# Decay of the state by small DMAs instead of column sums, with a new order of all engines, in a linear-attention and maxout kernel

## The chip, the cores and the metric

The kernel runs on one core of a Trainium2 chip. The metric is device time in microseconds (us) of one execution. Each quoted time is a median of several executions. A "step" below is the period of TensorE (PE) from one tile to the next, read between the transposes of x (`xtp`) of two neighbouring tiles.

## The reference, cut to what matters

A gated linear attention runs over 768 positions for 4 batches and 8 heads of 48 channels. Its output goes, as 3072 rows of 384, through a maxout layer of width 1024.

```python
f = 1.0 / (1.0 + np.exp(-f_logit))
for t in range(S):
    state = f[:, :, t, :, None] * state + np.einsum('bhd,bhe->bhde', k[:, :, t], v[:, :, t])
    y[:, :, t] = np.einsum('bhd,bhde->bhe', q[:, :, t], state)
x = y.transpose(0, 2, 1, 3).reshape(B * S, H * D)
out = np.maximum(x @ w1, x @ w2) @ w_out
```

## The kernel before

The sequence is cut into 6 chunks of 128 positions; chunk and batch make 24 tiles. For each tile the kernel forms `cum`, the running sum of -log f within the chunk, by one matmul with a triangle of ones. Then `ei` = exp(cum) scales k into `kp`, and `ed` = exp(-cum) scales q into `qp`. The state that goes into the next chunk is multiplied by the decay of the whole chunk, `fl`. It comes from column sums, four matmuls with one column each, which put the channels on partitions, where the state update wants them:

```python
    def p_cum(i):
        ...
        nc.tensor.matmul(out=ps[:, 0:dm], lhsT=ut, rhs=ell[:, :, 0:D], start=True, stop=True)
        for p in range(NP if i // B < nch - 1 else 0):
            nc.tensor.matmul(out=ps[:, dm + p:dm + p + 1], lhsT=ell[:, 2 * p:2 * p + 2, :]..., rhs=ones_col, ...)
    def a_ed(i):
        t = st[i]["ed"] = work.tile([C, dm], F32, name="ed", tag="ed")
        nc.scalar.activation(t, psum["cum", i][:, 0:dm], AF.Exp, scale=-1.0)
    def a_fl(i):
        ...
        nc.scalar.activation(t, psum["cum", i][:, dm:dm + NP], AF.Exp, scale=-1.0)
    def m_st(i):        # on GpSimd: new state = (old state + k'v) * fl
        ...
    def v_v(i):         # on VectorE: v to bf16
        nc.vector.tensor_copy(vb, ld[i]["v"].rearrange("p h d -> p (h d)"))
```

The order on every engine is written out by hand. A steady step is this list; a name is an operation and the number is its tile, relative to the current one. `lf`, `lk`, `lq`, `lv` are loads of 192 KB and `out` is a store, all issued by SyncE. `kpv` is kp on VectorE and `qp` is qp on GpSimd. `e` and `ln` make -log f. `tr` transposes kp and qp (copied to `trs`), `a` multiplies the two, `am` is `a` times the causal mask, `y` is am times v plus q times the old state, and `x` is y in bf16. `xT` transposes x, `d` is x times wd = w1 - w2, `g` its ReLU, and `o` the output row block, from g times w_out and x times w2o = w2 w_out, since max(a, b) = b + ReLU(a - b). `sa`, `tmp` and `st` update the state.

```python
STEP = """
st -4  d0 -1  cum 1  a 0  ed 1  d1 -1  g0 -1  am 0  lv 2  qp 1  fl 1  ei 1  lq 3  g1 -1
o0 -1  kpv 1  y 0  tmp -2  lk 3  o1 -1  x 0  e 2  xT 0  tr 1  ln 2  out -4  xTe 0  sa -1
tre 1  ob -1  lf 4  v 1
"""
```

A PROLOGUE and an EPILOGUE, written the same way, hold the first seven and the last few tiles.

## Time and profile before

| | kernel before |
|---|---|
| median of 3 runs | 146.11 us (146.02 to 146.57) |
| span of the profiled run | 144.2 us, granted clock 1.00 |
| step, middle and late | 4.98 and 4.90 us |
| busy: PE, VectorE (DVE), ScalarE (ACT), GpSimd (POOL) | 90%, 72%, 61%, 38% |

The prediction below shows the lines on which the reading of this kernel rests. The busy table of one stretch of the steady state (columns: stretch, length, then busy time and instruction count of each engine, granted clock, DMA share, GB/s):

```profile
85.00:120.00 35.00, 35.00 (x527) 28.35 (x525) 27.77 (x50) 23.60 (x57) 15.97 (x22) 1.00 0.98 206
```

PE is busy for all 35 us, and the DMA share is 0.98, at 206 GB/s. (The share adds up the times of all packets over 16 engines and can pass 1.) The list of DMA issues (columns: tiles, issuing engine, count, size, and median time from issue to landing):

```profile
ft<-in_f_logit_dram SPq DMA_DIRECT2D x24, 192.0 KB, 4.2
vt<-in_v_dram SPq DMA_DIRECT2D x24, 192.0 KB, 4.5
```

A load takes over 4 us from the start of its issue to its landing, although one is issued every us. So some four DMAs of SyncE's queue are under way at any time (3.4 on average, counted from the end of an issue; see below).

### The profile page before, as it was taken

Reading aid. Unit: us, or ns where it says so; the run is one execution under the profiler, and the core shown is the slowest. Engines: PE = TensorE matmul, PEld = TensorE weight load, DVE = VectorE, ACT = ScalarE, POOL = GpSimd, SP = SyncE. Lnnn points to the kernel's source line nnn. Section 1 sums busy time; section 2 is a strip of 40 time slices with the busy share of each in tenths; the row PEclk is TensorE's granted clock in tenths of the full one; section 3 lists DMA queues with packets and bytes.
Section 4 is the critical chain, followed back from the end, with each engine's and each line's share of the span. In section 5 each row is a group of like instructions: output and inputs, shape, how many; then the busy total and the mean of one; then the engine's idle time right before and its main releaser. Section 6 shows DMA issues by size and latency. Waiting matters only on the chain.

```text
span 144.2 us, 4442 instructions
## 1 busy us (share of the span) xinstructions
PE 130.0 (90%) x1820; PEld 101.3 (70%) x1820; DVE 104.4 (72%) x191; ACT 88.6 (61%) x199; POOL 54.6 (38%) x80
## 2 busy tenths in 40 slices
PE   0197499999899999999999999999999999999981
PEld 0044366677678877887887788778878877777771
DVE  7234988766989778877977797798779777976520
ACT  3572548877387566658566765766585667663440
POOL 8320060230556066236524632652364246362000
PEclk9999999999999999999999999999999999999999
DMA  4999999999999999999898999989899998971111
GB/s 93 271 362 386 341 303 154 188 188 140 206 174 196 188 213 221 173 227 233 166 203 183 215 208 210 219 181 196 182 198 222 190 251 180 225 223 57 59 55 55
DMA packets 104612, 28.60 MB, mean 198 GB/s; under 512 B 100368, under 2 KB 103568, under 8 KB 104592
## 3 DMA queue, kind: packets, MB, share of 16 engines
q1 hardware_dynamic: 104592, 28.32, 90.1%
q8 instruction: 14, 0.23, 0.7%
q14 instruction: 6, 0.05, 0.1%
HBM read 23.59 MB, written 4.72 MB: 196 GB/s over the span
## 4 chain that ended last, share of the span: by engine, by line
PE 72%; SPq 19%; DMA 4%; DVE 1%; issue 1%; ACT 0%
PE o L352 25%; PE d L334 22%; SPq L148 13%; PE tr L249 6%; PE a L267 5%; SPq L153 5%; DMA vt<-in_v_dram 4%; PE y L312 3%; PE y L307 2%; PE xtp L322 2%; PE cum L214 2%; PE sa L281 2%; SPq L157 1%; PE o L373 1%; DVE am L272 1%
## 5 line engine op out<-in xcount | busy, mean ns | idle before, releaser
L242 POOL TENSOR_TENSOR qp<-qt,ed 128x384 bf16<-128x384 f32 x22 | 22.3, 1013 | 61.7 <-ACT ed L226 31.6
L334 PE MATMUL d<-xT,wd 128*128 128x128 bf16 x576 | 40.6, 220 | 0.8 <-DVE xT L326 0.4
L352 PE MATMUL o<-wo,gT 128*128 128x384 bf16 x184 | 37.4, 325 | 0.0
L334 PEld LDWEIGHTS <-wd 128*128 128x128 bf16 x576 | 34.4, 114 | 3.8 <-DVE wd L175 0.6
L341 ACT ACTIVATE gT<-d 128x512 bf16<-128x512 f32 x48 | 29.0, 604 | 10.1 <-PE d L334 10.0
L272 DVE TENSOR_TENSOR am<-a,mask 128x1024 bf16<-128x1024 f32 x24 | 29.4, 1224 | 0.7 <-PE a L267 0.7
L296 POOL TENSOR_TENSOR st<-tmp,fl 64x192 bf16<-64x192 f32 x40 | 25.5, 638 | 1.6
L326 DVE COPY xT<-xtp 128x384 bf16<-128x384 bf16 x24 | 8.6, 358 | 21.1 <-PE xtp L322 21.1
L352 PEld LDWEIGHTS <-gT 128*128 128x128 bf16 x184 | 16.1, 97 | 9.1 <-ACT gT L341 0.2
L226 ACT ACTIVATE ed<-cum 128x384 f32<-128x384 f32 x24 | 11.8, 493 | 16.5 <-PE cum L216 13.1
L258 DVE COPY trs<-tr 128x1024 bf16<-128x1024 bf16 (+1 forms) x27 | 17.0, 631 | 2.9 <-PE tr L249 1.1
L317 ACT CAST x<-y 128x384 bf16<-128x384 f32 x24 | 11.5, 478 | 12.3 <-PE y L312 12.3
L352 PE MATMUL o<-w2o,xT 128*128 128x384 bf16 x69 | 15.0, 326 | 0.0
L201 ACT ACTIVATE e<-ft 128x384 f32<-128x384 f32 x24 | 12.5, 525 | 3.4 <-DMA ft<-in_f_logit_dram 3.4
L237 DVE TENSOR_TENSOR kp<-kt,ei 128x384 bf16<-128x384 f32 x23 | 14.1, 613 | 0.5 <-ACT ei L222 0.5
L214 PE MATMUL cum<-ell,ut 128*128 128x384 bf16 x24 | 8.1, 340 | 6.8 <-ACT ell L205 6.8
L205 ACT ACTIVATE ell<-e 128x384 bf16<-128x384 f32 x24 | 12.5, 524 | 0.7
L357 DVE COPY ob<-o 128x384 f32<-128x384 f32 x23 | 12.6, 548 | 0.0
L222 ACT ACTIVATE ei<-cum 128x384 f32<-128x384 f32 x24 | 12.1, 503 | 0.0
L312 PE MATMUL y<-vb,am 128*128 128x48 bf16 x192 | 11.3, 183 | 0.8 <-DVE am L272 0.6
L312 PEld LDWEIGHTS <-am 128*128 128x128 bf16 x192 | 9.6, 96 | 3.1 <-DVE am L272 1.4
L289 DVE TENSOR_TENSOR tmp<-sa,st 128x384 f32<-128x384 f32 x20 | 10.9, 546 | 0.0
(56 smaller groups left out, 167.6 us busy)
## 6 DMA issues: line engine op xcount, KB each, us to landing
ft<-in_f_logit_dram SPq DMA_DIRECT2D x24, 192.0 KB, 4.2
qt<-in_q_dram SPq DMA_DIRECT2D x24, 192.0 KB, 4.6
kt<-in_k_dram SPq DMA_DIRECT2D x24, 192.0 KB, 4.2
vt<-in_v_dram SPq DMA_DIRECT2D x24, 192.0 KB, 4.5
out_dram<-ob SPq DMA_DIRECT2D x23, 192.0 KB, 3.6
w_f<-in_moe_w_dram SPq DMA_DIRECT2D x6, 512.0 KB, 6.9
wo_f<-in_moe_w_out_dram SPq DMA_DIRECT2D x2, 768.0 KB, 8.4
out_dram<-obl SPq DMA_DIRECT2D x2, 96.0 KB, 1.6
```

The costliest lines, as they stand in the source:

```text
L148: nc.sync.dma_start(out=t, in_=SRC[name][b, :, sl, :].rearrange("h p d -> p h d"))
L201: nc.scalar.activation(e, ld[i]["f"].rearrange("p h d -> p (h d)"), AF.Exp, scale=-1.0)
L237: eng.tensor_mul(s["kp"][:, :, 0:D], ld[i]["k"], s["ei"].rearrange("p (h d) -> p h d", h=H))
L242: eng.tensor_mul(s["qp"][:, :, 0:D], ld[i]["q"], s["ed"].rearrange("p (h d) -> p h d", h=H))
L258: nc.vector.tensor_copy(s["tr"][:, n:n + len(sel)], psum.pop(("tr" + sel, i)))
L272: nc.vector.tensor_mul(am.rearrange("p o n c -> p (o n) c"), psum.pop(("a", i)).rearrange("p o n c -> p (o n) c"), mask)
L296: nc.gpsimd.tensor_mul(st_b[b][(c + 1) % 2][r, :, e], st[i]["tmp"][r, :, e], st[i]["fl"][r, :].unsqueeze(2).to_broadcast([DP, NP, D]))
L312: nc.tensor.matmul(out=y[:, ds], lhsT=am[:, o, p, :], rhs=vb[:, ds], start=(c == 0), stop=(c == 0 or o == 1))
L334: nc.tensor.matmul(out=ps[:, n, :], lhsT=wd[:, j, ff(f)], rhs=st[i]["xT"][:, j, :], start=(j == 0), stop=(j == JG - 1))
L341: nc.scalar.activation(s["g"][:, half * 4:half * 4 + 4, :], psum.pop(("d", half, i)), AF.Relu)
L352: nc.tensor.matmul(out=psum["o", i], lhsT=l() if callable(l) else l, rhs=r, start=(n == 0), stop=(n == len(mms) - 1))
L357: nc.vector.tensor_copy(t, psum.pop(("o", i)))
```

## The change

The intent is to take the column sums off PE. The decay equals the last row of `ed`, so from tile 5 on two small DMAs a tile copy that row (partition 127) to the partitions of the channels. For this `ed` is laid out anew, so that each channel's four values lie together. All orders are drawn anew: in the steady step `kp` goes to GpSimd and `qp` to VectorE. The first sixteen loads stay where they were, but for two.

```diff
 STEP = """
-st -4  d0 -1  cum 1  a 0  ed 1  d1 -1  g0 -1  am 0  lv 2  qp 1  fl 1  ei 1  lq 3  g1 -1
-o0 -1  kpv 1  y 0  tmp -2  lk 3  o1 -1  x 0  e 2  xT 0  tr 1  ln 2  out -4  xTe 0  sa -1
-tre 1  ob -1  lf 4  v 1
+lq 4  cum 1  d0 -1  ei 1  lk 4  a 0  kp 1  g0 -1  v 0  d1 -1  am 0  fd 0  ed 1  st -3  g1 -1
+o0 -1  lv 2  tmp -2  e 2  y 0  out -7  qpv 1  o1 -1  x 0  lf 4  ln 2  xT 0  tr 1  xTe 0
+sa -1  tre 1  ob -1
 """
+FIRST_MOVED = 5
 ... (PROLOGUE and EPILOGUE rewritten)
+    fl_b = [consts.tile([C, NP], F32, name=f"fl{n}") for n in range(NFL)]
-        for p in range(NP if i // B < nch - 1 else 0):
+        for p in range(NP if i < FIRST_MOVED else 0):
 ...
-        t = st[i]["ed"] = work.tile([C, dm], F32, name="ed", tag="ed")
-        nc.scalar.activation(t, psum["cum", i][:, 0:dm], AF.Exp, scale=-1.0)
+        t = st[i]["ed"] = work.tile([C, 2, D, NP], F32, name="ed", tag="ed", bufs=4)
+        nc.scalar.activation(t.rearrange("t h d p -> t p h d"), psum["cum", i]..., AF.Exp, scale=-1.0)
 ...
+    def move_fl(i):                                      # "fd"
+        if FIRST_MOVED <= i < (nch - 1) * B:
+            for h in range(2):
+                nc.sync.dma_start(out=fl_b[i % NFL][h * DP:h * DP + D, :],
+                                  in_=st[i]["ed"][C - 1:C, h].rearrange("o d p -> o (d p)"))
 ...
-        eng.tensor_mul(s["qp"][:, :, 0:D], ld[i]["q"], s["ed"].rearrange("p (h d) -> p h d", h=H))
+        eng.tensor_mul(s["qp"]...[:, :, :, 0:D], ld[i]["q"]..., s["ed"].rearrange("t h d p -> t p h d"))
```

More of the change, by code (lines that the diff above doesn't have):

```diff
@@ L17 @@
 PROLOGUE = """
-setup 0  setup 2  setup 1  lf 1  lf 0  lq 0  lw2 2  lk 0  lw2 0  lw2 1  lv 0  lwo 0  e 0
-lwo 1  e 1  ln 1  lk 1  ln 0  cum 0  cum 1  lw1 0  w2ca 2  warm 5  ei 0  lw1 2  fl 0  ed 0
-kp 0  ei 1  qpv 0  ed 1  fl 1  lw1 1  w2c 0  warm 3  warm 1  lq 1  w2ca 1  w2T 0  lf 2  w2T 7
-trk 0  w2Te 7  trq 0  w2T 4  trke 0  w2Te 0  trqe 0  w2T 5  w2T 1  a 0  lv 1  am 0  w2Te 1
-w2Te 4  v 0  lq 2  woc 2  w2T 2  y 0  w2Te 2  w2Te 5  woc 0  w2T 6  lk 2  w2T 3  woc 1  w2Te 6
-w2o 2  kpv 1  w2o 1  x 0  w2Te 3  trk 1  lf 3  wdp 0  woc 3  xT 0  trke 1  w2o 5  xTe 0
@@ L24 @@
-w2o 4  w2o 7  w2o 10  lv 2  w2o 8  w2o 0  sa 0  wd 2  w2o 11  w2o 3  lk 3  w2oe 2  w2o 6
-w2oe 1  w2o 9  wd 1  w2oe 0  lq 3  qpv 1  d1 0  lf 4  e 2  trq 1  d0 0  ln 2  trqe 1  tmp 0
-lf 5  a 1  g0 0  v 1  cum 2  am 1  ed 2  lv 3  o0 0  g1 0  qp 2  ei 2  y 1  fl 2  lq 4  kpv 2
-o1 0  x 1  xT 1  trk 2  xTe 1  lk 4  e 3  trq 2  trke 2  d0 1  ln 3  trqe 2  ob 0  lk 5
-cum 3  a 2  v 2  ed 3  d1 1  g0 1  am 2  lv 4  ei 3  g1 1  o0 1  kpv 3  lq 5  y 2  qp 3
-o1 1  x 2  fl 3  xT 2  lv 5  e 4  tr 3  xTe 2  ln 4  sa 1  d0 2  tre 3  lf 6  ob 1  cum 4
@@ L30 @@
-g0 2  a 3  d1 2  ed 4  lk 6  v 3  am 3  ei 4  g1 2  o0 2  lq 6  qp 4  e 5  tmp 1  y 3  fl 4
-o1 2  x 3  st 0  lf 7  kpv 4  ln 5  xT 3  tr 4  xTe 3  sa 2  lk 7  cum 5  tre 4  d0 3  ob 2
-a 4  lv 6  v 4  g0 3  d1 3  am 4  ei 5  ed 5  lv 7  g1 3  o0 3  qp 5  tmp 2  fl 5  y 4  kpv 5
-lq 7  o1 3  x 4  st 2  xT 4  lq 9  e 6  tr 5  xTe 4  st 1  sa 3  ln 6  d0 4  tre 5  lf 8
-ob 3  cum 6  g0 4  a 5  v 5  d1 4  ed 6  am 5  lq 8  ei 6  qp 6  g1 4  o0 4  tmp 3  fl 6
-out 2  e 7  y 5  kpv 6  o1 4  x 5  lk 8  ln 7  xT 5  tr 6  xTe 5  sa 4  lf 9  d0 5  tre 6
@@ L36 @@
-ob 4  cum 7  g0 5  a 6  out 0  v 6  d1 5  ed 7  am 6  ei 7  lv 8  qp 7  g1 5  o0 5  tmp 4
-y 6  kpv 7  out 1  o1 5  x 6  st 3  fl 7  xT 6  tr 7  lk 9  e 8  xTe 6  sa 5  ln 8  tre 7
-lk 10  ob 5  v 7  lf 10
+setup 0  setup 2  setup 1  lf 1  lf 0  lq 0  lw2 2  lk 0  lw2 0  lw2 1  e 1  lv 0  lwo 1
+e 0  lwo 0  ln 1  ln 0  lk 1  cum 0  cum 1  fl 0  warm 4  lw1 0  ed 1  ei 0  fl 1  ed 0
+lw1 2  w2ca 2  qp 0  warm 5  ei 1  lw1 1  w2c 0  kp 0  lq 1  w2ca 1  trk 0  trq 0  trke 0
+lf 2  v 0  w2T 7  w2T 6  w2T 2  w2Te 6  w2Te 7  trqe 0  w2T 3  w2Te 2  a 0  lv 1  w2T 4
@@ new lines @@
+w2T 1  sa 0  w2Te 4  w2Te 1  w2Te 3  am 0  w2T 0  lf 3  woc 1  w2Te 0  y 0  woc 0  w2T 5
+lk 2  kpv 1  w2Te 5  x 0  trk 1  tmp 0  w2o 0  woc 2  w2o 1  lq 2  wd 0  xT 0  woc 3  w2o 3
+w2o 2  w2o 6  lk 3  wd 2  w2o 4  w2o 5  w2o 7  w2o 8  xTe 0  w2o 9  lv 2  wd 1  w2o 11  w2oe 0
+w2o 10  w2oe 2  lq 3  qpv 1  w2oe 1  d0 0  trke 1  trq 1  lf 5  e 2  d1 0  trqe 1  g0 0
+a 1  ln 2  lf 4  v 1  g1 0  am 1  cum 2  ei 2  lv 4  o0 0  ed 2  fl 2  e 3  y 1  lv 3  kp 2
+o1 0  x 1  ln 3  xT 1  sa 1  cum 3  lq 4  qp 2  xTe 1  tmp 1  trk 2  ei 3  d0 1  trke 2
@@ new lines @@
+lk 4  kp 3  ob 0  trq 2  g0 1  d1 1  trqe 2  fl 3  lq 5  ed 3  v 2  a 2  g1 1  am 2  lk 5
+qp 3  o0 1  trk 3  st 1  trke 3  lf 6  e 5  y 2  trq 3  x 2  o1 1  trqe 3  ln 5  lv 5  e 4
+xT 2  a 3  xTe 2  ln 4  cum 5  ob 1  lf 7  d0 2  ei 5  v 4  ed 5  cum 4  g0 2  d1 2  lf 8
+v 3  am 3  fl 4  ed 4  g1 2  lq 7  qp 4  o0 2  ei 4  y 3  o1 2  fd 5  st 0  x 3  lk 6  kpv 4
+xT 3  tr 4  xTe 3  lq 6  qp 5  sa 2  sa 3  tre 4  d0 3  tmp 2  lk 9  a 4  g0 3  ob 2  d1 3
+st 2  am 4  lv 6  e 6  ln 6  o0 3  g1 3  kpv 5  lq 11  y 4  tmp 3  o1 3  x 4  lk 7  xT 4
@@ L39 @@
+tr 5  xTe 4  cum 6  d0 4  tre 5  ei 6  e 7  v 5  a 5  lq 9  ob 3  g0 4  d1 4  am 5  ed 6
+ln 7  lk 8  g1 4  o0 4  kpv 6  e 8  y 5  lv 7  qp 6  o1 4  x 5  lv 10  xT 5  tr 6  xTe 5
+sa 4  cum 7  fd 6  tre 6  lf 9  d0 5  ed 7  ob 4  ln 8  a 6  v 6  ei 7  lq 8  d1 5  am 6
+g0 5  g1 5  lf 10  kp 7  o0 5  qpv 7  y 6  tmp 4  o1 5  x 6  lv 8  st 4  xT 6  tr 7  xTe 6
+st 3  sa 5  cum 8  tre 7  d0 6  out 0  ob 5  a 7  g0 6  v 7  am 7  lk 12  lv 9  tmp 5  lk 10
+lq 10
 """
 STEP = """
-st -4  d0 -1  cum 1  a 0  ed 1  d1 -1  g0 -1  am 0  lv 2  qp 1  fl 1  ei 1  lq 3  g1 -1
@@ L43 @@
-o0 -1  kpv 1  y 0  tmp -2  lk 3  o1 -1  x 0  e 2  xT 0  tr 1  ln 2  out -4  xTe 0  sa -1
-tre 1  ob -1  lf 4  v 1
+lq 4  cum 1  d0 -1  ei 1  lk 4  a 0  kp 1  g0 -1  v 0  d1 -1  am 0  fd 0  ed 1  st -3  g1 -1
+o0 -1  lv 2  tmp -2  e 2  y 0  out -7  qpv 1  o1 -1  x 0  lf 4  ln 2  xT 0  tr 1  xTe 0
+sa -1  tre 1  ob -1
 """
 FIRST_STEP = 7
+FIRST_MOVED = 5
 EPILOGUE = """
-st 15  d0 18  cum 20  a 19  ed 20  d1 18  g0 18  am 19  qp 20  ei 20  lv 21  g1 18  o0 18
-tmp 17  st 16  out 15  y 19  kpv 20  o1 18  x 19  lk 22  e 21  xT 19  tr 20  ln 21  xTe 19
@@ L50 @@
-sa 18  d0 19  tre 20  lq 22  ob 18  cum 21  a 20  ed 21  v 20  lf 23  d1 19  g0 19  am 20
-qp 21  ei 21  g1 19  lv 22  o0 19  tmp 18  st 17  fl 21  out 16  y 20  kpv 21  o1 19  x 20
-lk 23  e 22  xT 20  tr 21  xTe 20  ln 22  sa 19  d0 20  tre 21  lq 23  ob 19  cum 22  lv 23
-a 21  ed 22  v 21  d1 20  g0 20  am 21  ei 22  out 17  g1 20  o0 20  tmp 19  fl 22  y 21
-out 18  qp 22  kpv 22  o1 20  x 21  st 18  xT 21  out 19  e 23  tr 22  xTe 21  ln 23  sa 20
-d0 21  tre 22  st 22  st 23  st 19  ob 20  cum 23  a 22  g0 21  v 22  d1 21  out 20  ed 23
@@ L56 @@
-am 22  ei 23  g1 21  o0 21  tmp 20  kpv 23  y 22  qp 23  o1 21  x 22  xT 22  st 20  st 21
-tr 23  xTe 22  sa 21  d0 22  tre 23  ob 21  a 23  g0 22  v 23  d1 22  out 21  am 23  g1 22
-o0 22  tmp 21  y 23  o1 22  x 23  xT 23  sa 22  xTe 23  ob 22  d0 23  out 22  d1 23  g0 23
-sa 23  g1 23  lo 0  lo 2  lob0 0  lo 1  fl 23  lo 3  lout 0  lob1 0  tmp 22  tmp 23  lout 1
+fd 21  fd 20  fd 22  fd 23  out 19  out 18  st 23  st 19  kp 23  out 20  st 21  st 22  st 20
+tr 23  o1 21  tre 23  xT 22  a 23  xTe 22  am 23  d0 22  d1 22  g0 22  ob 21  y 23  g1 22
@@ L60 @@
+tmp 22  out 21  x 23  o0 22  xT 23  o1 22  xTe 23  d0 23  ob 22  tmp 23  d1 23  out 22  g0 23
+sa 23  g1 23  lo 0  lo 2  lob0 0  lo 1  lo 3  lout 0  lob1 0  lout 1
 """
@@ L105 @@
     st_b = [[consts.tile([C, NP, 2 * D], BF16, name=f"st{b}_{n}") for n in range(2)] for b in range(B)]
+    NFL = 6
+    fl_b = [consts.tile([C, NP], F32, name=f"fl{n}") for n in range(NFL)]
     ut = consts.tile([C, C], BF16)
@@ L129, in setup @@
             nc.vector.tensor_copy(mask, ut.unsqueeze(1).to_broadcast([C, H, C]))
-            for t in kp_b[1:] + qp_b[1:]:
+            for t in kp_b[1:] + qp_b[1:] + fl_b:
                 nc.vector.memset(t, 0.0)
@@ L224, in a_ed @@
     def a_ed(i):
-        t = st[i]["ed"] = work.tile([C, dm], F32, name="ed", tag="ed")
-        nc.scalar.activation(t, psum["cum", i][:, 0:dm], AF.Exp, scale=-1.0)
+        t = st[i]["ed"] = work.tile([C, 2, D, NP], F32, name="ed", tag="ed", bufs=4)
+        nc.scalar.activation(t.rearrange("t h d p -> t p h d"), psum["cum", i][:, 0:dm].rearrange(
+            "t (p h d) -> t p h d", p=NP, h=2), AF.Exp, scale=-1.0)
     def a_fl(i):
@@ L230, in a_fl @@
             return
-        t = st[i]["fl"] = work.tile([C, NP], F32, name="fl", tag="fl", bufs=5)
-        nc.scalar.activation(t, psum["cum", i][:, dm:dm + NP], AF.Exp, scale=-1.0)
+        if i < FIRST_MOVED:
+            nc.scalar.activation(fl_b[i % NFL], psum["cum", i][:, dm:dm + NP], AF.Exp, scale=-1.0)
+    def move_fl(i):
[3 more added lines that the diff above has]
+                                  in_=st[i]["ed"][C - 1:C, h].rearrange("o d p -> o (d p)"))
     def m_kp(i, eng):
@@ L241, in m_qp @@
         s["qp"] = qp_b[i % NQ]
-        eng.tensor_mul(s["qp"][:, :, 0:D], ld[i]["q"], s["ed"].rearrange("p (h d) -> p h d", h=H))
+        eng.tensor_mul(s["qp"].rearrange("t (p h) d -> t p h d", h=2)[:, :, :, 0:D],
+                       ld[i]["q"].rearrange("t (p h) d -> t p h d", h=2), s["ed"].rearrange("t h d p -> t p h d"))
     def p_tr(i, sel):
@@ L296, in m_st @@
                 nc.gpsimd.tensor_mul(st_b[b][(c + 1) % 2][r, :, e], st[i]["tmp"][r, :, e],
-                                     st[i]["fl"][r, :].unsqueeze(2).to_broadcast([DP, NP, D]))
+                                     fl_b[i % NFL][r, :].unsqueeze(2).to_broadcast([DP, NP, D]))
     def p_y(i):
@@ L409 @@
         "g0": lambda i: a_g(i, 0), "g1": lambda i: a_g(i, 1),
-        "o0": lambda i: p_o(i, 0), "o1": lambda i: p_o(i, 1), "ob": v_ob, "out": store, "warm": warm,
+        "fd": move_fl, "o0": lambda i: p_o(i, 0), "o1": lambda i: p_o(i, 1), "ob": v_ob, "out": store, "warm": warm,
         "lo": p_last, "lob0": lambda n: ob_last(0), "lob1": lambda n: ob_last(1),
```

## The prediction

This text and the expectations below say "the lock" where an operation of VectorE and one of GpSimd overlap and one of them takes longer than it does alone. The trace of the kernel before has it near 130 us: kp on VectorE, 0.55 to 0.57 us in the steady steps, takes 0.89 us where it starts 0.53 us after qp on GpSimd. The word names that measured stretch; what in the hardware causes it is not shown.

> **What bounds the kernel now.** I read the page first (shares, then slices), then the chain of work that ended last, then the timeline of one middle step, one late step, the start and the end, and last the DMA counts by window.
>
> ```profile
> PE 130.0 (90%) x1820; PEld 101.3 (70%) x1820; DVE 104.4 (72%) x191; ACT 88.6 (61%) x199; POOL 54.6 (38%) x80
> PE   0197499999899999999999999999999999999981
> DMA  4999999999999999999898999989899998971111
> ```
>
> PE (TensorE) is full from about 18 us to 141 us, with one dent near 36 us, and the DMA engines are just as full from 4 to 130 us. Each is near its limit, so I priced both. The chain gives the period of PE. The same point of the step, the three transposes of x, ends its chain piece here in two middle steps and in two late ones:
>
> ```profile
> 102.70 0.17 PE xtp L322 x3
> 107.68 0.17 PE xtp L322 x3
> ...
> 117.56 0.17 PE xtp L322 x3
> 122.46 0.17 PE xtp L322 x3
> ```
>
> A middle step takes 107.68 - 102.70 = 4.98 us. A late one takes 122.46 - 117.56 = 4.90 us, and from tile 20 on a tile has no column sums (L216). So four one-column matmuls cost PE only 0.08 us a step. The timeline tells why it is so little (columns: start, busy time, engine, line). Middle step, then late steps:
>
> ```profile
> 89.06 0.33 PE L214 MATMUL cum<-ell,ut 128*128 128x384 bf16 x1
> 89.23 0.24 PE L216 MATMUL cum<-ones_col,ell 128*128 128x1 bf16 x4
> 89.40 0.40 PE L267 MATMUL a<-trs 48*128 48x128 bf16 x8
> ...
> 118.85 0.33 PE L214 MATMUL cum<-ell,ut 128*128 128x384 bf16 x1
> 119.11 0.40 PE L267 MATMUL a<-trs 48*128 48x128 bf16 x8
> ...
> 128.89 0.23 PEld L267 LDWEIGHTS <-trs 48*128 48x128 bf16 x8 [0.21 <-DVE trs L258]
> ```
>
> From the cum matmul to the first of `a` is 0.34 us with the sums and 0.26 us without, though cum itself passes in 0.17 us (89.06 to 89.23). `a` waits for DVE to copy the transposed k and q (`trs`, 0.69 us); the last line names that wait. The sums fill a gap that would be there anyway: 0.17 us of work bought back as 0.08.
>
> [...]
>
> ```profile
> 129.95 1.00 POOL L242 TENSOR_TENSOR qp<-qt,ed 128x384 bf16<-128x384 f32 x1 [1.27 <-issue]
> 130.48 0.89 DVE L237 TENSOR_TENSOR kp<-kt,ei 128x384 bf16<-128x384 f32 x1
> ```
>
> The DVE product, 0.55 us elsewhere, takes 0.89 where it starts under POOL's product and ends 0.42 us after it. [...]the new `ed` layout is read at a 16-byte step. No such read is in this trace. [...]
>
> **The change part by part.**
> 1. *Column sums.* Tiles 5 to 19 lose them: 15 x 4 = 60 matmuls and weight loads. At 0.08 us a tile this is 15 x 0.08 = 1.2 us on PE's path. Their 15 small exponentials leave ACT, 15 x 0.18 = 2.7 us, off the path since ACT is 61% busy.
> 2. *Thirty small DMAs.* Each writes 48 rows of 16 bytes; two a tile. They are issued after `ed` of the tile, and the state update that reads the result comes about three steps (15 us) later, so a landing of even 5 us is hidden. Their load is another matter. While loads alone run without SyncE waiting for anything (20 to 48 us), the 192 KB loads land one every 1.06 us: 22 of them between 22.0 and 45.1 us. That is 64 packets of 192 bytes on each of 16 engines, 16 ns each. A step's four loads need 4.2 us and a store about 0.4 us, 4.6 of 4.98 us. Six more packets an engine at the same 16 ns (an estimate from that rate) add 0.1 us: 4.7 of 4.90. Hidden, but with 0.2 us to spare.
> 3. *ed strided, kp to POOL, qp to DVE in the steady step.* DVE's step is am 1.22, trs 0.69, tmp 0.55, ob 0.55, xT 0.36, v 0.35, plus the product: 0.55 gives 4.27[...]. POOL does kp (1.0) and then the state (2 x 0.64) and is nearly through when the DVE product starts, so the lock should rarely bite. Path: 0.
> 4. *The end.* Before, d of the last tile stands idle for the copy of the last xT:
>
> ```profile
> 137.61 1.50 PE L334 MATMUL d<-xT,wd 128*128 128x128 bf16 x24 [0.45 <-DVE xT L326]
> ```
>
> The new order puts the last part of tile 22's o (0.81 us) between, so 0.45 us goes.
> 5. *The start.* The first sixteen loads keep their order but for the two halves of w_out. The first d needs all three wd, the last of which needs the last w1 load, landed near 20.5 us. Before, wd ran thus:
>
> ```profile
> 18.27 2.35 POOL L175 TENSOR_TENSOR wd<-w_f 128x1024 bf16<-128x1024 f32 x1 [8.29 <-DMA w_f<-in_moe_w_dram]
> 19.57 3.27 DVE L175 TENSOR_TENSOR wd<-w_f 128x1024 bf16<-128x1024 f32 x2
> ```
>
> The DVE pair began under POOL's and ended at 22.84, so one wd alone is (22.84 - 20.62) / 2 = 1.1 us. Now all three are on DVE, behind a longer queue: the first two products of tile 0 are both on POOL, one strided, so the transposes of tile 0 come about 0.3 us later, and I add up DVE's list (mask 1.22, w2T copies at 0.35, kp 0.55, tmp 0.55, xT 0.36, three wd at 1.1) to 23.3 us against 22.9 before. In the next 16 us four tiles interleave anew. Going through PE's list with the durations above, I find waits for x of tile 1 (ACT puts three exponentials ahead of it, 0.3 us), for POOL's qp 3 (0.15) and for g of tile 2 (exponentials of tiles 4 and 5 ahead of it, 0.3), against 0.6 us for am at 36 us saved. Net start: +0.6 us, give or take 1.0.
> 6. *Order of later loads.* q and v of tile 8 now stand behind k 9, q 11, q 9 and v 10. q 8 was the 27th load after f 2 (which landed at 23.0) and is now the 32nd. At 1.06 us, after v 1 at 24.6, that is 24.6 + 31 x 1.06 = 57.5 us, with two small DMAs ahead. Its product is due near 57.5 us, the old step's place plus the later start. I charge 0.3 us.
>
> Sum: -1.2 - 0.45 + 0.6 + 0.3 = -0.75, so 146.1 becomes about **145.3 us**.
>
> **Rivals.**
> - *DMA becomes the bound.* For it: the shares near 100%, and point 6. Against it: in a middle window the load queue stood at 93.9% where the saturated start, counted the same way, averaged about 105%, and SyncE had waits of its own. If a 16-byte write costs three times my figure, a step needs 4.6 + 0.3 = 4.9 us: level with PE. Beyond that, every 0.1 us is 1.2 us over the twelve steps left, less the slack of about 1.6 us that v 11 has: 145 to 147.
> - *DVE becomes the bound.* If the strided product takes over 1.1 us, or the lock adds 0.4 us a step, DVE needs 4.9 to 5.1 us and the steady steps lose all they gained and up to 0.1 us more: 146.5 to 148. For it: only 0.95 us of idle time a step now. Against it: POOL's turn ends before.
> - *PE wins all.* If `a` no longer waited for trs, a step would gain 0.17 instead of 0.08: 15 x 0.17 = 2.6 us, and with the end 3.0, just over 2%: 143.1. Against it: transpose, copy and `a` keep their distances. A better start than I count would also do it: the stalls between 11.5 and 24 us sum to about 3 us.
>
> **Range and chances.** The sure gains are 1.65 us and too small for 2% (2.9 us). Start and load order are worth plus or minus 1.5 us, the stride up to +2. Hence 143.5 to 147.4. Faster by over 2% needs a start better by over 1.3 us where I find it worse: 0.13. Slower by over 2% (149) needs a new bound in every step: 0.08. Else 0.79.
>
> **What would show it.** Steps of 4.90 us in the chain, with a wait of PE for trs before `a`: point 1 right; 4.8 or less: wrong. DVE's qp under 0.95 us and no wait of PE for qp: point 3. No wait of POOL for the small DMAs: point 2. No idle time before the last d: point 4. First d at about 23.3 us and the transposes of tile 3's x near 38.9 (37.8 before): point 5. A wait of DVE for q near 57 us: point 6. The prediction falls if a step comes out at 5.0 us or more, or if the start moves by over 1.5 us.

## The result, and the profile after

The changed kernel is correct and takes **158.57 us** (median of 4, 156.92 to 159.07), against 146.25 us (median of 4) for the kernel before on the same chip. The ratio of the two is 1.082, with a 95% interval of 1.073 to 1.091: slower by 8.2%, well outside the range predicted. A ratio here is the mean time of one kernel's fast runs over the mean of the other's from the same rounds, so it is not quite the ratio of the medians. The two profiled executions took 156.92 and 146.02 us, so the traces below hold 10.9 of the 12.3 us.

The page of the changed kernel, in the rows that answer to those of before (busy time and share by engine; then 40 slices of the span in tenths busy, and the granted clock of PE):

```profile
PE 135.8 (88%) x1760; PEld 100.5 (65%) x1760; DVE 119.9 (77%) x196; ACT 94.4 (61%) x184; POOL 54.0 (35%) x82
PE   0388699999999999999999999989989989979992
PEclk9999959999999999999999999999999999999999
DMA  5999999999979969977599879859759789597021
```

PE does 60 matmuls less, yet the row has dents in its last third. The DMA row, nines and eights before, falls to sevens, sixes and fives in many slices of its second half. If the transfers themselves were too heavy, one would expect the DMA engines to be as busy as before or busier. The stretch from 85 to 120 us says the same in numbers:

```profile
85.00:120.00 35.00, 32.11 (x445) 24.14 (x443) 30.86 (x46) 22.52 (x44) 13.44 (x20) 1.00 0.84 173
```

PE idles for 2.9 us, VectorE is busy for 3.1 us longer with four instructions fewer, and the DMA engines move 173 GB/s instead of 206.

Following `xtp` tile by tile through the trace gives the place of the loss (start of the transposes of x, us):

| tile | before | after | difference | step in the changed kernel, up to this tile |
|---|---|---|---|---|
| 3 | 37.80 | 39.80 | +2.0 | |
| 7 | 57.75 | 59.82 | +2.1 | 4.91 |
| 8 | 62.73 | 65.69 | +3.0 | 5.87 |
| 14 | 92.59 | 98.19 | +5.6 | 5.42, six times |
| 22 | 132.08 | 144.15 | +12.1 | 5.4 to 6.0, eight times |
| 23 | 136.83 | 147.61 | +10.8 | |

So there are four losses: 2 us at the start, 0.9 at tile 8, about 0.44 a step in tiles 9 to 14, and about 0.8 a step in tiles 15 to 22. The end gives 1.3 back.

**Tiles 9 to 14.** The chain of work that ended last, over one such step, then the timeline inside one of them (start, busy time, engine, line, tiles, and in brackets the idle time before and what ended it):

```profile
87.51 0.17 PE xtp L329 x3
...
92.93 0.17 PE xtp L329 x3
```

```profile
89.19 1.02 POOL L243 TENSOR_TENSOR kp<-kt,ei 128x384 bf16<-128x384 f32 x1 [3.25 <-issue]
89.23 1.19 DVE L206 CAST vb<-vt 128x384 bf16<-128x384 f32 x1
90.34 1.21 DVE L279 TENSOR_TENSOR am<-a,mask 128x1024 bf16<-128x1024 f32 x1
91.61 0.22 PE L319 MATMUL y<-vb,am 128*128 128x48 bf16 x2 [0.34 <-DVE am L279]
```

The step is 5.42 us. The cast of v takes 1.19 us where it took 0.35 before: it began 0.04 us after kp on POOL and ended 0.21 us after kp did. The mask product behind it comes late, and PE waits for that.

**Tiles 15 to 22.** The chain over late steps (100 to 124 us) has another face. Its line of totals comes first:

```profile
by line: DMA ft<-in_f_logit_dram 65.4%; ACT e L198 6.5%; PE d L341 6.2%; DVE am L279 5.0%; ACT x L324 4.7%; SPq L369 4.6%; PE xtp L329 4.4%; DVE qp L248 3.3%; DVE xT L333 3.1%; issue 2.0%; DVE tmp L296 1.9%; PE tr L256 1.9%; PE a L274 1.4%;
...
115.33 0.35 PE xtp L329 x3
121.00 0.36 PE xtp L329 x3
```

Loads of f carry two thirds of this chain, and the step is 5.67 us. From tile 15 or 16 on, f and v land when they are wanted and not before (ACT waits 10.5 us in all for f, in 11 pieces over the whole run), while k lands 7 us early and q 10. SyncE's own timeline, and the DMA share while it works at this, show why (a step has two small DMAs, `fl`):

```profile
99.46 1.04 SPq L145 DMA_DIRECT2D kt<-in_k_dram  x1
100.60 2.64 SPq L237 DMA_DIRECT2D fl<-ed  x2
103.29 0.58 SPq L145 DMA_DIRECT2D vt<-in_v_dram  x1
```

```profile
102.50:104.50 2.00, 1.82 (x26) 1.23 (x27) 1.30 (x3) 1.31 (x3) 0.00 (x0) 1.00 0.15 20
```

The two small DMAs hold SyncE for 2.64 us. The loads issued earlier run out meanwhile, the next can be issued only at 103.29, and from 102.5 to 104.5 us the DMA engines are 15% busy. Nothing that SyncE waits for on another engine explains it: `ed` of that tile had been ready for several us.

### The profile page after: what moved, and what is told of

Its sections match the earlier page's. It is cut to its first block, busy times and chain, and to the rows that moved or that the text cites. A ratio compares the mean times of both kernels' runs of the same rounds, so it can differ in the third digit from the quotient of the medians.

```text
span 155.1 us, 4425 instructions
## 1 busy us (share of the span) xinstructions
PE 135.8 (88%) x1760; PEld 100.5 (65%) x1760; DVE 119.9 (77%) x196; ACT 94.4 (61%) x184; POOL 54.0 (35%) x82
## 4 chain that ended last, share of the span: by engine, by line
PE 41%; DVE 19%; DMA 18%; ACT 7%; issue 6%; SPq 4%; POOL 2%; DVEq 0%
PE o L359 10%; DMA ft<-in_f_logit_dram 10%; PE d L341 10%; DVE am L279 8%; DMA vt<-in_v_dram 6%; PE tr L256 6%; PE w2op L189 3%; PE y L319 3%; SPq L237 2%; PE xtp L329 2%; DMA qt<-in_q_dram 2%; PE a L274 2%; ACT ed L225 2%; DVE mask L126 2%; PE cum L211 2%
## 5 line engine op out<-in xcount | busy, mean ns | idle before, releaser
L243 POOL TENSOR_TENSOR kp<-kt,ei 128x384 bf16<-128x384 f32 x20 | 20.7, 1035 | 67.8 <-ACT ei L219 25.8
L341 PEld LDWEIGHTS <-wd 128*128 128x128 bf16 x576 | 35.6, 114 | 3.5
L348 ACT ACTIVATE gT<-d 128x512 bf16<-128x512 f32 x48 | 29.7, 621 | 11.1 <-PE d L341 9.3
L303 POOL TENSOR_TENSOR st<-tmp,fl 64x192 bf16<-64x192 f32 x40 | 22.5, 563 | 4.2 <-DVE tmp L296 2.6
L225 ACT ACTIVATE ed<-cum 128x384 f32<-128x384 f32 x24 | 21.1, 880 | 1.5 <-PE cum L211 1.3
L206 DVE CAST vb<-vt 128x384 bf16<-128x384 f32 x24 | 18.5, 773 | 2.4 <-DMA vt<-in_v_dram 2.0
L198 ACT ACTIVATE e<-ft 128x384 f32<-128x384 f32 x24 | 12.6, 526 | 10.6 <-DMA ft<-in_f_logit_dram 10.5
L319 PEld LDWEIGHTS <-am 128*128 128x128 bf16 x192 | 9.1, 96 | 11.7 <-DVE am L279 11.3
L248 DVE TENSOR_TENSOR qp<-qt,ed 128x384 bf16<-128x384 f32 x18 | 15.7, 874 | 0.7 <-ACT x L324 0.7
```

Source lines behind the costliest of these rows:

```text
L198: nc.scalar.activation(e, ld[i]["f"].rearrange("p h d -> p (h d)"), AF.Exp, scale=-1.0)
L225: nc.scalar.activation(t.rearrange("t h d p -> t p h d"), psum["cum", i][:, 0:dm].rearrange("t (p h d) -> t p h d", p=NP, h=2), AF.Exp, sc ...
L243: eng.tensor_mul(s["kp"][:, :, 0:D], ld[i]["k"], s["ei"].rearrange("p (h d) -> p h d", h=H))
L248: eng.tensor_mul(s["qp"].rearrange("t (p h) d -> t p h d", h=2)[:, :, :, 0:D], ld[i]["q"].rearrange("t (p h) d -> t p h d", h=2), s["ed"]. ...
L303: nc.gpsimd.tensor_mul(st_b[b][(c + 1) % 2][r, :, e], st[i]["tmp"][r, :, e], fl_b[i % NFL][r, :].unsqueeze(2).to_broadcast([DP, NP, D]))
L319: nc.tensor.matmul(out=y[:, ds], lhsT=am[:, o, p, :], rhs=vb[:, ds], start=(c == 0), stop=(c == 0 or o == 1))
```

## The experiments

Times are medians in us. "Before" is the kernel before, run on the same chip in the same rounds, and the ratio is to it.

| run | edit | time | before | ratio (95%) |
|---|---|---|---|---|
| e1_sums | after, column sums again, no small DMA | 150.13 | 146.39 | 1.024 (1.017 to 1.031) |
| e2_v_on_act | after, v cast on ACT | 157.79 | 146.39 | 1.075 (1.067 to 1.083) |
| e12_sums_v_on_act | both | 148.04 | 146.39 | 1.008 (0.999 to 1.017) |
| e3_before_dma | before, with the small DMAs | 152.49 | 146.39 | 1.028 (1.015 to 1.040) |
| e8_fd_act_queue | after, small DMAs issued by ACT | 155.35 | 146.18 | 1.064 (1.060 to 1.067) |
| e9_fd_doubled | after, four small DMAs a tile | 180.41 | 146.18 | 1.232 (1.225 to 1.239) |
| e10_one_row | after, small DMAs as one row (wrong result) | 159.12 | 146.18 | 1.083 (1.076 to 1.090) |
| e11_before_dma_act | before, small DMAs issued by ACT | 146.96 | 146.18 | 1.003 (0.996 to 1.010) |
| e13_ei_later | e8, ei later | 152.89 | 145.98 | 1.046 (1.040 to 1.052) |
| e14_start | e13, qp of tile 0 on VectorE | 152.76 | 145.98 | 1.047 (1.041 to 1.053) |
| e15_before_act_dense | e11, issue at the end of the step, plain `ed` for tiles 0 to 4 | 145.74 | 145.98 | 1.000 (0.993 to 1.007) |
| e16_fd_late | e13, issue at the end of the step | 147.07 | 147.35 | 1.002 (0.994 to 1.009) |
| e17_am_first | e16, mask product of tile 0 earlier | 146.98 | 147.35 | 1.001 (0.995 to 1.008) |
| e18_fill | e16, start filled, DMA of tile 7 moved | 146.05 | 146.29 | 0.999 (0.995 to 1.003) |
| e19_before_fill | e15, start filled | 145.64 | 146.29 | 0.998 (0.994 to 1.002) |

In e3, e9, e10 and e11 one or two runs count as slow, because they lie over 1.5% above the fastest of their kernel. The ratios leave them out; the medians in the table do not. Of the fast runs alone e3 has a median of 150.7, e9 180.0, e10 158.8 and e11 146.4. The medians of before contain a slow run or two in the last two calls (rows e16 to e19; of its fast runs alone 146.3 and 146.2).

### Which part costs: e1, e2, e12, e3

The theories: (A) the lock of the v cast by kp, (B) the small DMAs that starve the load queue.

```diff
 e1:  -... am 0  fd 0  ed 1 ...          +... am 0  ed 1  fl 1 ...
      -FIRST_MOVED = 5                   +FIRST_MOVED = 20
 e2:  -... g0 -1  v 0 ...                +... g0 -1  va 0 ...      # va: nc.scalar.copy(vb, v)
 e3:  the kernel before, with move_fl, the new ed and FIRST_MOVED = 5:
      -... am 0  lv 2  qp 1 ...          +... am 0  fd 0  lv 2  qp 1 ...
```

> The changed kernel with the decay from the column sums again for all tiles (no small DMA), its order, its strided ed and its engines kept. Theory A, lock: kp on POOL stretches the v cast on DVE from 0.35 to some 1.1 us and delays the mask product; this alone makes the steps of tiles 8 to 22 5.4 us, so the time stays at about 156.5 to 158.5. Theory B, small DMAs: each takes SyncE 0.5 to 2 us to issue and leaves the load queue empty, so f and v come late; then steps 15 to 22 fall from 5.7 to 5.4 at least (154.5), and if B is the whole cause and the lock only follows from late v, to 4.9 (about 147.5). Both together: 153.5 to 155, with steps of 5.4 and the load slack back at 2 us or more.

> The changed kernel with the v cast of tiles 7 on done by ACT instead of DVE[...]. Lock alone: steps 9 to 22 fall to 4.9, 14 times 0.5 = 7 us less, 151.5. Small DMAs alone: nothing moves, 158. Both: tiles 9 to 14 get steps of 4.9, then the late loads bind earlier and the steps are set by SyncE's 5.4 to 5.8 us for seven issues: 154 to 156.5.

> Both edits at once. If lock and small DMAs are the whole of the loss in the steady steps: steps of about 4.9 to 4.98 throughout, and what is left is the start (+2.0) less the end (-1.3) against the kernel before: 146.5 to 148.5. If a third cause sits in the new order (strided ed on ACT and DVE, loads of q and k ahead of f and v), steps stay at 5.1 or more: 150 or more.

> The kernel before, in its own order, with only the decay moved to the small DMAs for tiles 5 on (strided ed with it). Small DMAs hold up the load queue whatever the order: loads lose their 3 to 4 us of slack by tile 15 or so, then steps of 5.3 to 5.7: 148.5 to 152. Small DMAs harmless and only the new order at fault: 144.5 to 146 (column sums gained 1.2). Strided ed at fault: POOL's qp 1.19 us instead of 1.0 and ACT's ed 0.88: steps of 5.0 to 5.1 from the first steady tile on, with loads in time.

*Measured.* Giving the sums back to PE (e1) wins 8.4 us of the 12.3. That is more than "both together" allowed, and fits none of the ranges: most steps fall to 5.02, not to 5.42. From tile 12 on, f and v land 4.4 us or more ahead of use. Moving the v cast alone (e2) wins 0.8, which is within the spread of the runs: steps of 4.9 appear in tiles 10 and 11, and then the loads bind earlier, with single steps up to 6.95. Its total misses the range for "both" (154 to 156.5) and lies at that for the small DMAs alone (158). Both edits leave 148.04, inside the range expected, with steps of 5.02, and of 4.91 where a tile has no sums. The kernel before with small DMAs (e3) takes 152.5 (its two fast runs 149.9 and 151.6): its steps are 4.90 to 4.95 in tiles 6 to 11; from tile 12 on f and v land just as they are wanted, k and q with 0.1 to 0.3 us to spare, and steps of 4.9 and up to 6.2 follow in turns.

*What follows.* The small DMAs alone are enough to spoil the old order too, so B is the main cause and not the order of loads. The changed kernel, e1, e2 and e12 give the sizes: with the v cast on ACT, where it takes 0.51 us (mean) in both e2 and e12, the small DMAs cost 9.8 us (e2 against e12); without small DMAs the lock, which bites in e1 only in tiles 8 and 19 to 22, costs 2.1 us (e1 against e12). The lock is real, but costs little while the loads bind. It explains the 5.42. e1 shows by how little it is missed. The cast and kp in one of its steps of 5.02:

```profile
86.50 0.35 DVE L206 CAST vb<-vt 128x384 bf16<-128x384 f32 x1
86.53 1.19 POOL L243 TENSOR_TENSOR kp<-kt,ei 128x384 bf16<-128x384 f32 x1 [2.78 <-issue]
```

Here the cast starts 0.03 us *ahead* of kp. Now the cast is short and kp takes 1.19 us, which harms nobody. In the changed kernel kp starts 0.04 us ahead, and the cast takes 1.19. The tail of e1, where tiles have no sums, falls back to that: there kp is again 0.04 to 0.05 us ahead and the steps are 5.41. The column sums had delayed `ei`, and so kp, just enough. That is how e1 won more than expected.

### Why thirty tiny DMAs starve the loads: e8, e9, e10, e11

Counting in the traces from the end of an issue to the landing, SyncE's queue holds on average 3.4 DMAs between 85 and 120 us before, and 3.3 after. The total hardly moves, but of the 3.3 only 2.6 are loads and stores; small DMAs are the other 0.7. In e1 the loads and stores are back at 3.5. An issue that holds SyncE up for long ends with few others in flight. Of the issues of over 0.8 us between 20 and 130 us, before has 58, of which 39 end with three others in flight, 16 with two and 3 with four; after has 48, with 35, 11 and 2. (The text on record for e8 says "nearly always exactly three"; mostly three, often two, is right.) So the theory is that the queue takes some four DMAs at once whatever their size. That is inferred from these counts; what the runs below test is its consequence, that the number of DMAs costs, and not their load. The same sum by bare issue time does not explain it: the shortest issues in the trace after, 0.42 (f), 0.45 (q), 0.43 (k), 0.44 (v), 0.33 (store) and twice 0.52 (small), with 0.5 for gaps, make 3.6 us of a step of 5.7.

```diff
 e8:  -                nc.sync.dma_start(out=fl_b...      +                nc.scalar.dma_start(out=fl_b...
 e9:  each of the two DMAs of a tile split in two of 24 rows
 e10: -out=fl_b[i % NFL][h * DP:h * DP + D, :]            +out=row_b[i % NFL][h * DP:h * DP + 1, :]
 e11: e3 with nc.scalar.dma_start
```

> The changed kernel with the thirty small DMAs issued by ACT, on its own queue, instead of SyncE. In the first two kernels and in the runs so far an issue on SyncE that is held up ends nearly always when exactly three DMAs, of whatever size, are still in flight before it. Theory slots: SyncE's queue takes about four DMAs at once, and a small one holds a place for 2 to 4 us like a large one; on another queue they take none of those places, loads come in time again, and what is left is the lock and the start: 148.5 to 151. Rival, the DMA engines themselves (16-byte writes cost more than their packets show): 156 or more, f and v late again. Rival, ACT: two issues of 0.5 us a step make ACT late: steps of 5.2 or more with PE waiting for x or g.

> The changed kernel with four small DMAs a tile of 24 rows each instead of two of 48: same bytes, same packets, twice the count. Theory slots: the landings of a step's seven DMAs sum to about 23.4 us, over four places 5.85 us a step; two more of 2.3 us make 28 us, 7.0 us a step. From tile 9 on, some 14 steps of 7.0 instead of 5.6, so 170 to 178. Bytes or packets at fault: 157 to 160, as nothing is added.

> The changed kernel, wrong on purpose: each small DMA writes its 768 bytes as one row of a scratch tile instead of 48 rows of 16 bytes, so the decays stay zero. Same count of DMAs and bytes, no scattered 16-byte writes. Theory slots (the count matters): within 2% of the changed kernel, 155 to 159, and f and v late as there. If the 48 scattered writes are the cost: 150 to 152, like the kernel with column sums.

> The kernel before with the decay by small DMAs (its own order, strided ed), but issued by ACT on its own queue. Theory slots: the late loads of e3_before_dma vanish, steps of 4.93 to 4.98 to the end, 145 to 147. If small DMAs slow the transfers themselves: 149 to 153 as e3_before_dma.

*Measured.* Doubling the count at the same bytes (e9) costs 22 us more; its steps from tile 9 to 21 are 5.9 to 9.4 and average 7.15, against 7.0 expected. It overshoots the total, 180.4 against 170 to 178, since the loads bind from tile 6 on. Writing 768 bytes as one row instead of 48 scattered pieces (e10) changes nothing: 159.1, with f and v as late. Thus the scattered writes do not matter, and at equal bytes the count does. On ACT's queue the small DMAs harm no load: in e11 every load has 2.6 us of slack or more from tile 9 on, all steps but two are 4.90 to 4.95 from there, and the time falls from 152.5 to 147.0 (fast runs: 150.7 to 146.4). The strided `ed` is the same in both, so it is not what slows e3. In e8 loads are early again as well (v by 3.8 us or more from tile 11 on).

But e8 as a whole misses its range: 155.35 against 148.5 to 151. Its steps stand at 5.42, and the timeline says why:

```profile
89.24 1.01 POOL L243 TENSOR_TENSOR kp<-kt,ei 128x384 bf16<-128x384 f32 x1 [3.25 <-DMA fl<-ed]
89.28 1.18 DVE L206 CAST vb<-vt 128x384 bf16<-128x384 f32 x1
```

With the loads in time the lock sits in nearly every step. I had allowed it no more than it cost in e1. The third rival, two issues that make ACT late with steps of 5.2 or more, fits 5.42 as well; e13 separates the two and finds both.

What no run separates is what the limit is: a number of DMAs that one queue holds, or some fixed time of each DMA that the next ones on its queue must wait out.

### The lock, and ACT's issues: e13, e16

```diff
 e13 (on e8): -d0 -1  ei 1  lk 4  a 0  kp 1  g0 -1  v 0     +d0 -1  lk 4  a 0  g0 -1  ei 1  kp 1  v 0
 e16 (on e13): -am 0  fd 0  ed 1 ... sa -1  tre 1           +am 0  ed 1 ... sa -1  fd 1  tre 1
               -ln 8  a 6  (PROLOGUE)                      +ln 8  fd 7  a 6
```

> The small DMAs on ACT's queue as in e8, and one word moved in the steady step: ei of the next tile behind the first half of g on ACT, so that kp on POOL starts some 0.6 us later. In e8 kp started 0.04 us ahead of the v cast in nearly every step and the cast took 1.18 us; in e1 it started 0.03 us behind and the cast took 0.35. Theory lock: with kp well behind, the cast takes 0.35 in every steady step, steps fall from 5.42 to about 4.91, 14 of them: 7 us, so 148 to 150. If the 5.42 has another cause (ACT busy with DMA issues, DVE full): 153 or more.

> e13 with ACT's two DMA issues moved from ahead of ed to the end of the step, where ACT waits for cum in any case. In e13 the steps with small DMAs take 5.24 and the two without them 4.91; the theory is that the 1.1 us of issues holds up ed and, behind it, the second half of g, which PE's o waits for. Then all steps fall to 4.91, 13 times 0.33, 4.3 us less than e13 (152.9): about 148.5, that is the kernel before plus the start (2.0 to 2.5), less 1.1 for the sums, plus some 0.9 for tiles 8 and 22. If the steps stay at 5.2, the DMAs or ACT's total are at fault, and 152 to 153.

*Measured.* In e13 kp starts 1.05 us after the cast, and the cast takes 0.35 us in every step from tile 8 on: the lock of the cast is gone by order alone. (It moves in part to qp, which now meets the state update on GpSimd and takes 1.05 to 1.19 us in most steps; PE does not wait for that.) Yet the time is 152.89, out of its range, with steps of mostly 5.24, except that tiles 20 and 21, which have no small DMA, take 4.91. ACT spent 1.1 us a step on two DMA issues ahead of `ed` and the second half of g, for which PE's o waits (from one step: ACT's two issues, `ACTq`, `ed` behind them, and the weight load that waits for g):

```profile
94.17 0.57 ACTq L237 DMA_DIRECT2D fl<-ed  x1
94.78 0.60 ACTq L237 DMA_DIRECT2D fl<-ed  x1
95.43 0.88 ACT L225 ACTIVATE ed<-cum 128x384 f32<-128x384 f32 x1 [0.29 <-issue]
96.79 0.44 PEld L359 LDWEIGHTS <-gT 128*128 128x128 bf16 x4 [0.28 <-ACT gT L348]
```

With the issues at the end of the step (e16) every steady step is 4.91 us, and the time is 147.07, 5.8 us less; 4.3 was expected of the steps, and the profiled run was 1.5 us earlier at tile 3, where the two programs are the same. The stretch of e16 that answers to those shown before and after:

```profile
85.00:120.00 35.00, 35.00 (x511) 28.15 (x509) 30.09 (x51) 23.57 (x49) 18.33 (x22) 1.00 1.04 199
```

PE is full again, and this is the step that the prediction had promised.

### The start: e14, e17, e15, e18, e19

```diff
 e14 (on e13): -w2ca 2  qp 0  warm 5                         +w2ca 2  qpv 0  warm 5
 e17 (on e16): -sa 0  w2Te 4  w2Te 1  w2Te 3  am 0  w2T 0 ... y 0    +sa 0  am 0  y 0  w2Te 4  w2Te 1  w2Te 3  w2T 0
 e18 (on e16): -w2Te 0  y 0                                  +w2Te 0  ws 5  y 0     # ws: unread matmuls
               -qp 0  warm 5                                 +qp 0  warm 7
               -ln 8  fd 7  a 6 ... cum 8  tre 7             +ln 8  a 6 ... cum 8  fd 7  tre 7
 e19 (on e15): -woc 2  w2T 2                                 +woc 2  ws 6  w2T 2
 e15 (on e11): -am 0  fd 0  lv 2 ... ln 2  out -4            +am 0  lv 2 ... ln 2  fd 1  out -4
               -ln 8  tre 7  (PROLOGUE)                      +ln 8  fd 7  tre 7     # and plain ed for tiles 0 to 4
```

> e13 with the product qp of tile 0 on DVE instead of POOL, so that kp 0 need not queue behind a strided product of 1.19 us and be stretched to 1.44. Theory: the transposes of tile 0 come 1 to 1.5 us earlier, and of the 1.5 to 2.0 us by which the start is late at tile 3 about 1 us is won: 147 to 148.8. Rival: the start is set by the late mask product and the half clock of TensorE near 18 to 22 us, whatever tile 0's products do: no change against e13.

> e16 with one repair of the start: the mask product of tile 0 ahead of three w2T copies on DVE, and y of tile 0 ahead of one w2T on PE, as the kernel before had it. In the changed kernel PE stands 1.33 us for it near 17 us and the granted clock falls after that. Theory: x of tile 0 about 1 us earlier and the start at tile 3 0.7 to 1.2 us better than in e16, 147.5. Rival, as in e14: what is won there is lost again in the wait for the last wd on DVE or for the weights, no change against e16.

> A version meant to be good: the kernel before in its own order, decay of tiles 5 on by small DMAs on ACT's queue, issued at the end of a step where ACT waits for cum anyway, and the plain ed layout for tiles 0 to 4, so that the start is as before. Steps of 4.90 instead of 4.98 from tile 5 on: 1.1 us less than the kernel before, 145 against 146.2; 1 us more if ACT's issues are held up as in three steps of e11.

> e16 with the wait of PE for the mask product of tile 0 filled by five matmuls whose result nobody reads (and two more while it waits for kp of tile 0), and the DMAs of tile 7 issued by ACT after the step's other work, which held up g by 1.0 us in e16. Theory clock: the half clock near 18 to 22 us follows from PE standing idle between 12 and 17 us; with the gaps filled the granted clock stays at 1.0, the start improves by 0.5 to 1 us, and the mended tile 6 gives 1.0 more: 145 to 145.9 against e16's 147.1. Rival: the clock falls in spite of it; then only tile 6 is won, 146.0 to 146.5.

> e15 with six such matmuls in the 1.58 us that PE waits near 15 us for the mask product of tile 0. The kernel before kept the full clock there, its variant e15 did not in its profile (start 1.1 us later at tile 1). Theory clock: the start is that of the kernel before in every run and the steps of 4.90 show in the end: 145.0 to 145.3, 0.6 to 0.8% under the kernel before. Rival: fillers delay real work by as much as they win: 145.7 to 146.3.

*Measured.* Neither an earlier product of tile 0 (e14) nor an earlier mask product (e17) moves the time: what they win is waited for again, in e14 for the cast of the third weight (1.47 us), in e17 for k of tile 1 (PE idle 1.36 us). The fillers do keep the clock. The row of the granted clock in e18, where the changed kernel had a five:

```profile
PEclk9999999999999999999999999999999999999999
```

In the twelve runs of e18 and e19 the mean clock is 0.996 to 1.0; of the eleven runs of before in the same rounds nine are at 0.974 to 0.988. But the time does not follow. e18 reaches tile 3 at 38.76 us, e16 at 38.80; what e18 wins is tile 6, whose step falls from 5.99 to 4.97 because my own misplaced DMA issue of tile 7 is gone; 0.4 of it is lost again in the next step (5.32 against 4.90). Its 146.05 lies in the range of its rival, which had expected the clock to fall; the clock did not. Runs of before with a clock of 0.984 and 1.0 took 145.37 and 145.47. So the half clock near 20 us accompanies the late start, and is not shown to cause it.

e15 and e19 were meant to beat both kernels. Most of their steps are 4.90, and their ratios are 1.000 and 0.998, both intervals containing 1; both miss the 145 to 145.3 that was expected. In the profiles e15 is 0.3 us later than before at tile 7 and 0.7 us quicker from there to tile 22; e19 has two steps of 5.2 and 5.3. No version here is shown to be faster than the kernel before.

## Why the prediction was wrong

**Point 2, the small DMAs, failed, and it is the main miss.** "Hidden, but with 0.2 us to spare" priced packets: 0.1 us a step. That price was right. On ACT's queue in e8 the packets of the thirty small DMAs can be told apart (queue, packets, MB, share of 16 engines' span):

```profile
q10 hardware_dynamic: 1920, 0.02, 0.7%
```

That is 1.1 us of 154, or 0.07 us a tile (1920 packets are eight an engine and tile, not six). What was left out is that each small DMA is under way on SyncE's queue for 2.9 us (the median from issue to landing, as against 3.7 for a load of v), however little it carries. From the end of its issue it took 2.1 us (median) to land, and no such time was in the sum. The sum that should have been made is DMAs in flight: five a step of 4.98 us, some 3.4 us each from the end of the issue, are 3.4; with two more of 2.1 us in 4.90 us they would be 4.3, on a queue that held 3.3 to 3.7 on average in before, after, e1 and e3. The rival "DMA becomes the bound" came nearest, but for too much traffic, with 145 to 147. It came with too little: 173 GB/s. Removing the small DMAs is worth 8.4 us in e1, part of it by the lock, and 9.8 us where the cast is on ACT (e2 to e12).

**Point 3, the lock, failed.** "The lock should rarely bite" looked only at qp on DVE. It does hold for qp in the changed kernel: 0.84 to 0.90 us from tile 8 on, below the 0.95 allowed, and PE waits for it only at tile 8. The cast of v, which in the new order stands beside kp, was not checked. The lock bit there in all steps of tiles 8 to 14. Which of the two starts first decided it in these runs: with kp 0.03 us behind the cast (e1) the cast takes 0.35 us, with kp 0.04 us ahead (e8) it takes 1.18, and the step (5.42 us in e8) is 0.4 to 0.5 us longer. The second rival named the right size ("the lock adds 0.4 us a step"), but for VectorE's total, and at 146.5 to 148.

**Point 5, the start, was mis-sized.** It was put at +0.6, give or take 1.0; at tile 7 it measured +2.1 in the profile after, +1.35 in e1 and +1.2 in e18. The first d began at 24.74, not at 23.3:

```profile
21.82 1.21 DVE L172 TENSOR_TENSOR wd<-w_f 128x1024 bf16<-128x1024 f32 x1
...
24.74 0.44 PE L341 MATMUL d<-xT,wd 128*128 128x128 bf16 x5
```

The last wd is done at 23.0, near the 23.3 that I had added up; it is PE that is late, with the matmuls of w2o (`w2op`) at half clock: from 20 to 22 us the granted clock is 0.50, and `w2op` matmuls start 0.320 us apart, against 0.162 in before. For 128 columns this trace has 0.107 us from start to start (`xtp` at 19.8 us) and 0.056 at full clock (`tr` at 18.8 us). But as e18 shows, restoring the clock did not bring the start back. The profiles of all runs with this same start (after, e1, e2, e8, e9, e10, e12, e13, e16) reach tile 3 between 1.0 and 2.5 us later than before; what makes it vary stays open.

**Point 6, the load order, was mis-sized**: q of tile 8 landed at 59.70 us instead of 57.5, with four small DMAs (of tiles 5 and 6) ahead of it where the prediction counted two, and PE waited:

```profile
60.71 0.40 PE L256 MATMUL tr<-ident,qp 128*128 128x128 bf16 x4 [0.34 <-DVE qp L248]
```

The step of tile 8 is 0.9 us longer than one of before, but the lock has its part in it (e1, with q in time, still takes 5.43).

**Points 1 and 4 were right in direction, less so in their reasons.** Without the column sums and with no other wait a step is 4.91 us, in tile 7 of the changed kernel and throughout in e16: the 4.90 predicted. But the wait of `a` for trs that was to show it is not there, since in the new order half of d stands between cum and `a`; with the sums that order has 5.02 (e1, e12; no wait of PE in e1's steps), so there they cost 0.11 and fill no gap. In the old order the wait shows (e15, up to 0.2 us before `a`, steps of 4.90). At the end the last d no longer stands idle for xT; o of tile 22, from 147.78 us, lies before it:

```profile
148.59 1.50 PE L341 MATMUL d<-xT,wd 128*128 128x128 bf16 x24
```

Yet from tile 21 to the end the changed kernel takes 16.89 us and e16 16.78, against 17.01 before: 0.1 to 0.2 won and not 0.45, because the new order makes the step to tile 22 longer (5.59 in e16).

So the steps were priced well, the end and the start less well, and the two missing terms were the queue and the lock. The chance of 0.08 for "a new bound in every step" was set by looking at PE, VectorE and bytes; the change put new work on the one queue whose issues were already held up (58 issues of over 0.8 us before).

## What to carry to other kernels

Price a DMA in two currencies: the bytes it moves, and the time it is under way on its queue from issue to landing. On SyncE's queue, which feeds loads without a break, a tiny DMA was under way nearly as long as a large one (2.9 us against 3.7), and twice as many at the same bytes cost 22 us (e9 against after). Issue it on another engine's queue, at a point where that engine waits anyway (e16, 147.07 us, against 152.89 in e13). Look at every VectorE operation that can meet a GpSimd one, casts included (here 1.19 us instead of 0.35), and put them clear of each other (in e13 kp starts 1.05 us after the cast, which stays at 0.35), because here 0.04 us decided it, and a matmul removed elsewhere was enough to tip the order.

## What the runs show of the queue, the lock, the stride and the clock

- The bare issue times in the changed kernel left SyncE 2 us a step (3.6 of 5.7). Still, in fast runs the same thirty small DMAs cost some 4 us on SyncE's queue (e3, ratio 1.028) and 0.4 us, within the noise, on ACT's (e11, 1.003).
- The mean number of DMAs in flight on SyncE's queue, counted from the end of an issue to the landing, is 3.3 to 3.5 in before, after and e1, whatever the sizes, and issues of over 0.8 us end with two to four others in flight, mostly three (before and after). What in the hardware sets this is not shown.
- Of the cast and kp, the one that started second took longer, by less than what was left of the first. A cast of 0.35 us that started 0.04 us after kp (after) ended 0.21 us after kp did, so 0.84 more where 0.98 of kp were left; kp, started 0.03 us after such a cast (e1), took 1.19 us instead of 1.0, so 0.19 more where 0.32 of the cast were left. (Spans on GpSimd are rough in these profiles.)
- The new `ed` is read at a step of 16 bytes. GpSimd's qp with one such operand of two took 1.20 us in e3 against 1.01 before, 19% more.
- With the same step, VectorE's qp took 0.85 us (after, median) instead of 0.54 (before, at 22.8 us), and ACT's write of `ed` 0.88 (after) instead of 0.49 (before).
- Half clock came at 19.3 us in after, where PE had had gaps of no more than 0.9 and 1.3 us near 11 and 17 us, while the profile of before kept full clock after one of 1.6 near 14.5 us. With the wait of PE for the mask product filled (e18, e19) the mean clock was 0.996 or above in twelve runs. How long a gap must be for half clock is not shown.
